# A fused attention, MLP and soft-MoE kernel: the MLP rows of five batches turned by VectorE and DMA for the routing logits

## The chip, the cores and the metric

The kernel runs on one core of a Trainium2 chip. A core has engines that each run their own instruction stream in order and wait for one another by semaphores: TensorE (PE, matmuls and transposes), VectorE (DVE), ScalarE (ACT), GpSimd (POOL) and SyncE (SP, which here issues the DMAs). The metric is the device time of one execution in microseconds (us), the median of the runs.

## The reference

Inputs are f32. Three parts follow one another.

```python
# attention with a small state: x [8,8,512,64], state [8,8,32,64]  (batch, head, token/slot, 64)
a     = softmax(x @ state^T / 8);  xread = a  @ state     # per token, over 32 slots
a2    = softmax(state @ x^T / 8);  sread = a2 @ x         # per slot, over 512 tokens
x     = concat([xread, sread], tokens)                    # -> 8*(512+32) = 4352+256 = 4608 rows of 512

# gated MLP, 512 -> 1536 -> 512
xn    = x / sqrt(mean(x*x) + 1e-6) * rms_g
h     = silu(xn @ w_gate) * (xn @ w_val)                  # [4608,1536]
x     = h @ w_out

# soft MoE: 8 experts with 4 slots each, 32 slots in all
logits = x @ phi                                          # [4608,32]
d      = softmax(logits, over all tokens);  slot_in = d^T @ x
out_e  = relu(slot_in_e @ w1_e) @ w2_e
c      = softmax(logits, over the 32 slots);  result = c @ slot_out
```

## The kernel before

The MLP's output x = h @ w_out is never formed. The kernel folds w_out into phi (`wphi` = w_out @ phi, 1536 x 32), so that logits = h @ wphi, and it sums d^T @ h for the slots, with w_out applied once at the end. The sum over tokens goes batch by batch with a running maximum (`mrun`, `al`, `acc`).

The work is staged by batches of 512 tokens. Stages 0 and 1 work on batches 0 and 1, with the preparation of weights. Then each stage from 2 to 7 is one batch, with 12 units: three chunks c of 512 MLP columns by four tiles t of 128 tokens. A unit is a gate group of six 128x512 matmuls (`main_mm(.., 0)`), silu by ScalarE into `sg` (L496), a value group of six matmuls, and `h` = value x scale x sg by VectorE (L504). Groups write PSUM buffers of the pool `mm` (four); all other products and transposes go through `misc` (three), the logits through `lg` (one). Beside the units, the same engines carry for the next batch its attention: `sT` (token scores), softmaxes (`a`, asum, `e2T`), state reads; the conversion of w_out from its input words (`raw` to `wo` by ScalarE, VectorE and GpSimd, written to DRAM as `w_out`); and the weights of the next chunk times the state (`sw`: `misc<-w,stTg` on TensorE, `wp` by ScalarE L467 and VectorE L468).

The logits need h with its 512 columns on the partitions, since TensorE contracts over the partitions. `h` has tokens there. So `h_T` (L509 to 517) makes four 128x128 transposes on TensorE for a tile (L109), into one misc buffer, which ScalarE copies to `hT` (in units 1 and 2 of a stage VectorE does, L515). Once the four tiles of a chunk are there, `lg_mm` (L519 to 534) multiplies four 128x32 pieces of wphi with the four pieces of hT, each into its own 32 partitions of `lg`, summed over the three chunks. After the last chunk of a batch `post1` copies lg to `lgs`, `post2` sums the four pieces by a matmul and updates the running maximum (`L`, `cmx`), `post_exp` takes the exponential (`E`, `al`), `post3` turns E and L (`ET`, `c_all`), and `slot_h` adds d^T @ h (`misc<-h,ET`).

The order: each unit asks `next_turned` for up to two tiles that are ready (`pend`), turns them and multiplies; `at(u, slot, f)` writes a function into a plan at a unit and one of two slots, and `run(slot)` plays it. The framework's scheduler then orders each engine's stream from that program, so that what is written later may stand earlier. SyncE's DMAs are issued in order from one queue. Big tiles (`h`, `hT`, `raw`, `xT`, ...) come from one pool `k8` of 19 buffers of 128x2048 f32; a tile that takes a buffer waits until the last user of it is done.

## Time and profile before

| | |
|---|---|
| runs, median (lowest to highest) | 671.63 us (671.53 to 674.0) |
| the profiled execution | 673.21 us, its span 671.4 us, clock 0.968 |
| TensorE busy | 622.3 us, 93% of the span, 4448 instructions |
| VectorE busy | 402.4 us, 60% |
| ScalarE busy | 354.8 us, 53% |
| GpSimd busy | 161.2 us, 24% |
| DMA | 92.54 MB, mean 138 GB/s |
| transposes of h on TensorE (L109, with others) | 61.1 us listed, 408 of them |
| gate and value groups (L85, mm) | 307.3 us listed, 1152 matmuls |
| hT copies by ScalarE (L515) | 49.5 us, 86 of them |

Busy is the sum of an engine's instruction times. Matmuls overlap in the pipeline, so what one costs is read from the distance between starts rather than from its own time. The span is the profiled part of one execution; the execution's own time has 1.8 us more. [...] The chain that ended last goes 68% over TensorE, 17% over VectorE, 6% over ScalarE and 3% over DMA.

### The profile page before, as it was taken

What the parts mean: (1) busy time and instruction counts of PE and PEld (TensorE: products, weight loads), DVE (VectorE), ACT (ScalarE), POOL (GpSimd) and SP (SyncE); (2) the same over time, 40 slices, a digit from 0 to 9 for tenths busy, and PEclk for the clock granted to TensorE, in tenths of its full rate; (3) what the DMA queues carried; (4) which work ended last, traced back from release to release, by engine and by line L of the source; (5) the groups of instructions that cost most, each with busy time, mean ns of one, the idle gap of its engine ahead of it and who ended that gap; (6) DMA issues with size and microseconds to landing.
All of it is one profiled execution on the core that took longest, in us unless ns stands there. A gap on an engine that the chain in (4) does not pass through costs nothing.

```text
span 671.4 us, 11241 instructions
## 1 busy us (share of the span) xinstructions
PE 622.3 (93%) x4448; PEld 393.5 (59%) x4448; DVE 402.4 (60%) x831; ACT 354.8 (53%) x599; POOL 161.2 (24%) x172
## 2 busy tenths in 40 slices
PE   6786989999999999999999999999999999999880
PEld 4344556546656766576676657666666777643350
DVE  6969898675398366646835673584554266242170
ACT  5466784566466547445744645485445576211170
POOL 2635364542044003302310340221000000014320
PEclk9698998999999999999999999999899999999995
DMA  9950065132013203202110320300363037999767
GB/s 348 405 221 1 1 250 189 63 130 67 1 49 145 68 0 130 101 1 91 70 68 3 125 95 1 126 6 28 125 252 126 0 120 256 312 355 386 265 228 304
DMA packets 33580, 92.54 MB, mean 138 GB/s; under 512 B 1912, under 2 KB 4088, under 8 KB 30712
## 3 DMA queue, kind: packets, MB, share of 16 engines
q1 hardware_dynamic: 33240, 91.76, 37.3%
q8 instruction: 35, 0.57, 0.4%
q14 instruction: 17, 0.14, 0.1%
q10 hardware_dynamic: 288, 0.07, 0.0%
HBM read 79.76 MB, written 12.06 MB: 137 GB/s over the span
## 4 chain that ended last, share of the span: by engine, by line
PE 68%; DVE 17%; ACT 6%; DMA 3%; issue 2%; POOL 1%; DVEq 0%; POOLq 0%; ACTq 0%
PE mm L85 38%; PE misc L85 18%; PE misc L109 7%; PE lg L85 3%; DMA ew<-in_w_dram 2%; DVE w L208 2%; DVE h L504 2%; DVE asum L322 1%; DVE w L204 1%; DVE wp L468 1%; DVE w L200 1%; ACT sT L298 1%; DVE wo L208 1%; ACT wp L467 1%; ACT a L311 1%
## 5 line engine op out<-in xcount | busy, mean ns | idle before, releaser
L85 PE MATMUL mm<-wp,A 128*128 128x512 f32 x1152 | 307.3, 407 | 2.2 <-ACT sg L496 1.2
L85 PEld LDWEIGHTS mm<-wp,A 128*128 128x128 f32 x1152 | 206.9, 190 | 91.9 <-issue 49.3
L504 DVE SCALAR_TENSOR_TENSOR h<-mm,rinv,sg 128x512 f32<-128x512 f32 x102 | 75.5, 743 | 85.9 <-PE mm L85 78.8
L496 ACT ACTIVATE sg<-mm,rinv 128x512 f32<-128x512 f32 x102 | 70.6, 692 | 81.0 <-PE mm L85 67.3
L467 ACT CAST wp<-misc 128x512 fp32r<-128x512 f32 x96 | 51.8, 590 | 77.2 <-PE misc L85 77.2
L468 DVE TENSOR_TENSOR wp<-misc,wp 128x512 fp32r<-128x512 f32 x96 | 62.0, 684 | 50.5 <-ACT wp L467 50.4
L85 PE MATMUL misc<-w,stTg 64*32 64x512 f32 x768 | 67.5, 627 | 11.2 <-POOL w L212 6.8
L515 ACT COPY hT<-misc 128x512 f32<-128x512 f32 x86 | 49.5, 584 | 39.2 <-PE misc L109 33.1
L109 PE MATMUL misc<-ident,h 128*128 128x128 f32 x408 | 61.1, 275 | 3.7 <-DVE h L504 2.2
L109 PEld LDWEIGHTS misc<-ident,h 128*128 128x128 f32 x408 | 48.0, 140 | 23.3 <-issue 4.1
L85 PE MATMUL misc<-bd,A 128*128 128x256 f32 x192 | 32.1, 306 | 4.4 <-DVE wp L468 2.2
L85 PEld LDWEIGHTS misc<-w,stTg 64*32 64x32 f32 x768 | 11.0, 106 | 42.7 <-POOL w L212 16.7
L212 POOL TENSOR_TENSOR w<-w,raw 128x512 int32<-128x512 int32 x20 | 28.2, 1422 | 30.1 <-issue 9.0
L85 PEld LDWEIGHTS misc<-bd,A 128*128 128x128 f32 x192 | 27.3, 203 | 9.9 <-DVE wp L468 2.6
L441 POOL TENSOR_TENSOR rinv<-ri,rs_magic 128x4 int32<-128x4 int32 (+1 forms) x9 | 1.8, 198 | 130.2 <-DVE ri L437 130.2
L422 ACT ACTIVATE misc<-misc 128x512 f32<-128x512 f32 x32 | 18.7, 584 | 25.7 <-PE misc L85 24.2
L85 PE MATMUL mm<-wh,xsg 128*128 128x512 f32 x96 | 31.7, 399 | 0.0
L212 POOL TENSOR_TENSOR wo<-wo,raw 128x512 int32<-128x512 int32 x18 | 24.3, 1364 | 26.3 <-DVE wo L208 22.1
L269 POOL TENSOR_TENSOR a<-a,rm 128x1024 f32<-128x1024 f32 x7 | 13.4, 1916 | 62.6 <-issue 58.1
L1089 POOL MEMSET sinE<- 128x512 f32 x2 | 1.0, 524 | 111.4 <-PE mm L85 101.2
L325 POOL TENSOR_TENSOR a<-a,asum 128x1024 f32<-128x1024 f32 x7 | 13.4, 1917 | 59.4 <-DVE cs L640 50.1
L85 PE MATMUL lg<-hT,wphi 128*32 128x512 f32 (+1 forms) x216 | 27.5, 578 | 0.0
(203 smaller groups left out, 844.7 us busy)
## 6 DMA issues: line engine op xcount, KB each, us to landing
ew<-in_w_dram SPq DMA_DIRECT2D x27, 1024.0 KB, 7.9
xT<-in_x_t_dram SPq DMA_DIRECT2D x8, 1024.0 KB, 5.1
xn<-in_x_n_dram SPq DMA_DIRECT2D x8, 1024.0 KB, 6.8
raw<-in_w_val_dram SPq DMA_DIRECT2D x6, 1024.0 KB, 16.6
raw<-in_w_out_dram SPq DMA_DIRECT2D x6, 1024.0 KB, 4.9
out_dram<-ob SPq DMA_DIRECT2D x6, 1024.0 KB, 12.9
ew_w<-in_w_dram SPq DMA_DIRECT2D x5, 1024.0 KB, 12.0
raw<-in_w_gate_dram SPq DMA_DIRECT2D x4, 1024.0 KB, 14.3
```

Of the source, the lines that this page charges most:

```text
L85: nc.tensor.matmul(out=o, lhsT=lhsT, rhs=rhs, start=start, stop=stop)
L109: nc.tensor.transpose(o, i, ident)
L208: nc.vector.scalar_tensor_tensor(out=a[:, h], in0=hi[:, h], scalar=-0x40000000, in1=a[:, h], op0=ALU.bitwise_and, op1=ALU.bitwise_or,)
L212: nc.gpsimd.tensor_tensor(out=a[:, h], in0=a[:, h], in1=rnd[:, h], op=ALU.add)
L269: nc.gpsimd.tensor_tensor(out=a3, in0=a3, in1=rm.unsqueeze(2).to_broadcast([P, 32, 32]), op=ALU.subtract)
L325: (eng or nc.gpsimd).tensor_tensor(out=a3, in0=a3, in1=asum.unsqueeze(2).to_broadcast([P, 32, 32]), op=ALU.mult)
L422: nc.scalar.activation(out=ps, in_=ps, func=AF.Square, accum_out=T[b, "ss"][:, t : t + 1])
L467: nc.scalar.copy(t[:, r, 0, :], ps)
L468: nc.vector.tensor_tensor(out=t[:, r, 1, :], in0=ps, in1=t[:, r, 0, :].bitcast(F32), op=ALU.subtract)
L496: nc.scalar.activation(out=sg, in_=ps, func=AF.Silu, scale=RINV[g][:, t : t + 1])
L504: nc.vector.scalar_tensor_tensor(out=HH[g, c][:, t, :], in0=ps, scalar=RINV[g][:, t : t + 1], in1=sg, op0=ALU.mult, op1=ALU.mult,)
L515: (nc.vector.tensor_copy if on_dve else nc.scalar.copy)(HT[g, c][:, :, t * P : (t + 1) * P], ps.rearrange("p (q n) -> p q n", q=4))
```

## The change

For batches 2 to 6 the rows of h are turned without TensorE. `next_turned` hands out two tiles of one chunk at a time. `h_blocks` has VectorE transpose 32x32 blocks of the two tiles (128x1024) into a tile `hB`, with the blocks regrouped so that partition p holds 32-column pieces by block row. When both halves of a chunk are there, `h_move` writes hB by one DMA to a DRAM tile `hD` (1 MB, three buffers) and reads it back by four DMAs of 256 KB, each into 32 partitions of `hT`, which puts the blocks on the partitions where a whole transpose has them. `lg_end` multiplies as before, planned three units later, and reads hT in runs of 32 elements; for the last chunk of a batch it plans `post1` to `slot_h` behind itself. Batches 0, 1 and 7 and the state rows stay with TensorE's transposes.

```diff
--- before.py
+++ after.py
@@ -133,6 +133,7 @@
 
     dram = ctx.enter_context(tc.tile_pool(name="dram", bufs=1, space=bass.MemoryType.DRAM))
     w_out32 = dram.tile([DFF, DM], F32, name="w_out32")
+    hdram = ctx.enter_context(tc.tile_pool(name="hdram", bufs=1, space=bass.MemoryType.DRAM))
     bits = {
         0: w_gate.bitcast(I32), 1: w_val.bitcast(I32), 2: w_out_t.bitcast(I32),
         3: w_out.bitcast(I32),
@@ -516,22 +517,54 @@
             HT[g, c][:, :, t * P : (t + 1) * P], ps.rearrange("p (q n) -> p q n", q=4)
         )
 
+    def by_dma(g):
+        return 2 <= g < B - 1
+
+    HB = {}
+
+    def h_blocks(g, c, t):
+        if t == 0:
+            HB[g, c] = k8("hB")
+        nc.vector.transpose(
+            HB[g, c].rearrange("p g (x i) -> p x g i", i=32)[:, 4 * t : 4 * t + 8],
+            HH[g, c][:, t : t + 2, :].rearrange("p t (q g i) -> p (t q) g i", q=4, g=4),
+        )
+
+    def h_move(g, c):
+        hB = HB.pop((g, c))
+        hT = k8("hT")
+        D = hdram.tile([P, 4, 512], F32, tag="hD", bufs=3, name=f"hD_{g}_{c}")
+        nc.sync.dma_start(out=D, in_=hB)
+        for g_ in range(4):
+            nc.sync.dma_start(
+                out=hT[32 * g_ : 32 * g_ + 32],
+                in_=D[:, g_, :].rearrange("(b i) r -> i b r", b=4),
+            )
+        HT[g, c] = hT.rearrange("p b (t q i) -> p t q b i", q=4, i=32)
+
+    def lg_part(g, c, hT, n):
+        if c == 0:
+            LGP[(g,)] = psp.tile([P, 512], F32, tag="lg", bufs=1, name="lg")
+        lg = LGP[(g,)]
+        for q in range(4):
+            mm(
+                lg[32 * q : 32 * q + 32, : n * P],
+                wphi[:, 4 * c + q, :],
+                hT(q),
+                start=(c == 0),
+                stop=(c == NC - 1),
+            )
+
+    def lg_moved(g, c):
+        hT = HT.pop((g, c))
+        lg_part(g, c, lambda q: hT[:, :, q], NT)
+
     def lg_mm(g, c, t):
         n = gsize(g)
         if t < n - 1:
             return
-        if c == 0:
-            LGP[(g,)] = psp.tile([P, 512], F32, tag="lg", bufs=1, name="lg")
-        lg = LGP[(g,)]
         hT = HT.pop((g, c))
-        for q in range(4):
-            mm(
-                lg[32 * q : 32 * q + 32, : n * P],
-                wphi[:, 4 * c + q, :],
-                hT[:, q, : n * P],
-                start=(c == 0),
-                stop=(c == NC - 1),
-            )
+        lg_part(g, c, lambda q: hT[:, q, : n * P], n)
 
 
     sacc = small("sacc", [P, 1])
@@ -813,6 +846,8 @@
     def next_turned():
         pend.sort()
         now = [it for it in pend[:2] if it[1] in wphi_done and it[0] == pend[0][0]]
+        if now and by_dma(now[0][0]):
+            return now if len(now) == 2 and now[0][1] == now[1][1] else []
         return [] if now and now[0][1:] == (0, 0) and now[0][0] > 0 and now[0][0] - 1 not in ended else now
 
     ended = set()
@@ -823,6 +858,19 @@
             ended.add(now[-1][0])
         return end
 
+    def after_lg(pg, v):
+        ended.add(pg)
+        for u, slot, f in ((0, 2, post1), (1, 1, post2), (1, 1, post_exp), (2, 2, post3)):
+            plan.setdefault((v + u, slot), []).append((f, (pg,)))
+        for i in range(NC):
+            plan.setdefault((v + 4, 1), []).append((slot_h, (pg, i)))
+
+    def lg_end(g, c):
+        lg_moved(g, c)
+        if c == NC - 1:
+            after_lg(g, unit[0])
+
+    unit = [0]
     for s, units in enumerate(stages):
         def at(u, slot, f, *a):
             plan.setdefault((base + u, slot), []).append((f, a))
@@ -948,27 +996,31 @@
 
         for u, (g, c, t) in enumerate(units):
             def run(slot):
-                for f, a in plan.pop((base + u, slot), []):
-                    f(*a)
-
+                while fs := plan.pop((base + u, slot), []):
+                    for f, a in fs:
+                        f(*a)
+
+            unit[0] = base + u
             now = next_turned()
             ps = main_mm(g, c, t, 0)
             sg = main_silu(g, c, t, ps)
+            moved = now and by_dma(now[0][0])
             for it in now:
-                h_T(*it, on_dve=(s > 0 and u in (1, 2)))
+                if not moved:
+                    h_T(*it, on_dve=(s > 0 and u in (1, 2)))
             run(1)
             psv = main_mm(g, c, t, 1)
             main_h(g, c, t, psv, sg)
-            for it in now:
-                lg_mm(*it)
-            if ends(now):
-                pg = now[-1][0]
-                at(u, 2, post1, pg)
-                at(u + 1, 1, post2, pg)
-                at(u + 1, 1, post_exp, pg)
-                at(u + 2, 2, post3, pg)
-                for i in range(NC):
-                    at(u + 4, 1, slot_h, pg, i)
+            if moved:
+                h_blocks(*now[0])
+                if now[1][2] == NT - 1:
+                    h_move(*now[1][:2])
+                    at(u + 3, 2, lg_end, *now[1][:2])
+            else:
+                for it in now:
+                    lg_mm(*it)
+                if ends(now):
+                    after_lg(now[-1][0], base + u)
             run(2)
             pend = pend[len(now) :] + [(g, c, t)]
             if g == B - 2 and u == len(units) - 1:
```

Three places in the order show what moves. On TensorE, at the start of batch 4's stage around the attention transposes (`sT`); before, with A the batch's rows, wp its weights and `misc<-ident,h` the transposes of h:

```order
L85 MATMUL mm<-wp_2894,A_2595 128x512 x6
L85 MATMUL misc<-w_557,stTg 32x512 x8
L85 MATMUL mm<-wp_2839,A_2595 128x512 x6
L109 MATMUL misc<-ident,h_3005 128x128 x4
L85 MATMUL mm<-wp_2894,A_2595 128x512 x6
L109 MATMUL misc<-ident,sT 128x128 x8
L599 MATMUL misc<-ident,E 128x128
L600 MATMUL misc<-ident,L 128x128
L85 MATMUL mm<-wp_2839,A_2595 128x512 x6
L85 MATMUL mm<-wp_2894,A_2595 128x512 x6
L85 MATMUL mm<-wp_3011,A_2595 128x512 x5
```

Here a transpose block of h stands between two groups, and the eight matmuls of w_557 stand together. After the change, the same place of the program (`lg<-hT` of the batch before stands just ahead of it):

```order
L109 MATMUL misc<-ident,sT 128x128 x4
L85 MATMUL mm<-wp_2919,A_2500 128x512
L109 MATMUL misc<-ident,sT 128x128 x4
L85 MATMUL misc<-lgs,r_75 32x128 x4
L85 MATMUL mm<-wp_2919,A_2500 128x512 x3
L85 MATMUL mm<-wp_2955,A_2500 128x512 x6
L85 MATMUL misc<-w_677,stTg 32x512 x4
L85 MATMUL mm<-wp_2919,A_2500 128x512
L85 MATMUL misc<-w_677,stTg 32x512 x4
L85 MATMUL mm<-wp_2919,A_2500 128x512 x5
L85 MATMUL mm<-wp_2955,A_2500 128x512
L85 MATMUL misc<-xn_2945,e2T 32x64 x32
```

The transposes of h are gone, those of E and L no longer stand here, the state-write group of w_677 is in two halves around one gate matmul, and the matmuls on `e2T` come ahead of the value group's rest.

On VectorE, at the same place; before, from the row maximum `cmax` of post3 to the next stage of h:

```order
L606 TENSOR_REDUCE cmax<-misc 128x4
L643 RECIPROCAL cs<-cs 128x4
L504 SCALAR_TENSOR_TENSOR h_3005<-mm,rinv,sg 128x512
L644 TENSOR_TENSOR c_all<-c_all,cs 128x128
L200 TENSOR_SCALAR wo_3133<-wo_3133 128x512 x2
L204 TENSOR_SCALAR wo_3133<-wo_3133 128x512 x2
L208 SCALAR_TENSOR_TENSOR wo_3133<-raw_3044,wo_3133 128x512 x2
L335 COPY e2T<-misc 128x512
L607 TENSOR_TENSOR c_all<-misc,cmax 128x128
L504 SCALAR_TENSOR_TENSOR h_3005<-mm,rinv,sg 128x512
L394 STREAM_TRANSPOSE aT<-a 128x1024
L504 SCALAR_TENSOR_TENSOR h_3235<-mm,rinv,sg 128x512
```

Three h's stand among these rows, and each conversion step (L200, L204, L208) is done for both halves at once. After, from the reciprocal of asum to the second h (`h_3098` is the chunk that starts with unit 4; `h_2909`, of units 0 to 3, stands ahead of this piece, then two `hB` transposes):

```order
L673 TENSOR_SCALAR cs<-cs 128x4
L205 TENSOR_SCALAR wo_3007<-wo_3007 128x512
L676 RECIPROCAL cs<-cs 128x4
L201 TENSOR_SCALAR wo_3007<-wo_3007 128x512
L677 TENSOR_TENSOR c_all<-c_all,cs 128x128
L209 SCALAR_TENSOR_TENSOR wo_3007<-raw_2943,wo_3007 128x512
L205 TENSOR_SCALAR wo_3007<-wo_3007 128x512
L336 COPY e2T<-misc 128x512
L209 SCALAR_TENSOR_TENSOR wo_3007<-raw_2943,wo_3007 128x512
L395 STREAM_TRANSPOSE aT<-a 128x1024
L593 COPY L<-misc 128x128
L594 TENSOR_REDUCE cmx<-misc 128x1
L505 SCALAR_TENSOR_TENSOR h_3098<-mm,rinv,sg 128x512
```

No h stands here any more until L and cmx of the batch before are read, and e2T has come between the two L209.

On SyncE, at the start of a stage; before:

```order
L120 DMA st<-in_st_n_dram 128x128
L162 DMA raw_3044<-in_w_out_dram 128x2x1024
L126 DMA xn_3046<-in_x_n_dram 128x2048
L219 DMA w_out_89<-wo_3133 128x2x512
L119 DMA stT<-in_st_t_dram 128x128
L118 DMA xT_3431<-in_x_t_dram 128x2048
```

Nothing but a small state load stands ahead of `raw`. After, at the same place:

```order
L537 DMA hD_2_2913<-hB_2860 128x2048
L120 DMA st<-in_st_n_dram 128x128
L539 DMA hT_2912<-hD_2_2913 32x4x512 x4
L163 DMA raw_2943<-in_w_out_dram 128x2x1024
L126 DMA xn_2945<-in_x_n_dram 128x2048
L537 DMA hD_0_3102<-hB_3005 128x2048
L220 DMA w_out_89<-wo_3007 128x2x512
L539 DMA hT_3101<-hD_0_3102 32x4x512 x4
L118 DMA xT_3305<-in_x_t_dram 128x2048
```

The loads of `raw` and `xn` now come behind the write of hD and the four reads of hT of the chunk that ended the batch before.

## Rows read from the trace of the kernel before

**Rows 1.** Busy time by window, batch 5; columns: busy, clock, DMA share, GB/s

```profile
373.00:432.40 59.40, 58.90 (x463) 38.80 (x463) 35.77 (x75) 32.62 (x59) 12.44 (x11) 1.00 0.18 63
```

**Rows 2.** TensorE's timeline, start of batch 5; start, length, idle before

```profile
372.95 1.06 PE L85 MATMUL lg<-hT,wphi 128*32 128x512 f32 x8
373.95 1.09 PE L85 MATMUL misc<-w,stTg 64*32 64x512 f32 x16
...
376.46 0.60 PE L109 MATMUL misc<-ident,h 128*128 128x128 f32 x4
376.99 0.43 PE L85 MATMUL misc<-lgs,r 128*32 128x128 f32 x8
...
381.45 0.60 PE L109 MATMUL misc<-ident,h 128*128 128x128 f32 x4
381.81 1.63 PE L85 MATMUL mm<-wp,A 128*128 128x512 f32 x6
383.27 1.04 PE L109 MATMUL misc<-ident,sT 128*128 128x128 f32 x8
...
391.85 0.63 PE L109 MATMUL misc<-ident,h 128*128 128x128 f32 x4 [0.38 <-DVE h L504]
```

**Rows 3.** VectorE's timeline, the same stretch

```profile
375.70 1.29 DVE L468 TENSOR_TENSOR wp<-misc,wp 128x512 fp32r<-128x512 f32 x2 [0.92 <-ACT wp L467]
377.10 0.69 DVE L515 COPY hT<-misc 128x512 f32<-128x512 f32 x1
...
382.70 0.16 DVE L315 TENSOR_SCALAR rs<-s 128x2 f32<-128x2 f32 x1
...
383.53 1.22 DVE L322 TENSOR_REDUCE asum<-a 128x32 f32<-128x1024 f32 x1 [0.48 <-ACT a L311]
...
388.96 1.28 DVE L208 SCALAR_TENSOR_TENSOR wo<-raw,wo 128x512 int32<-128x512 int32 x2
390.17 0.68 DVE L335 COPY e2T<-misc 128x512 f32<-128x512 f32 x1
390.77 0.28 DVE L607 TENSOR_TENSOR c_all<-misc,cmax 128x128 f32<-128x128 f32 x1
390.96 0.74 DVE L504 SCALAR_TENSOR_TENSOR h<-mm,rinv,sg 128x512 f32<-128x512 f32 x1
391.62 1.23 DVE L394 STREAM_TRANSPOSE aT<-a 128x1024 f32<-128x1024 f32 x1
```

**Rows 4.** ScalarE's timeline, the same stretch

```profile
377.37 1.28 ACT L585 ACT_TABLE_LOAD   x1
...
380.07 1.08 ACT L467 CAST wp<-misc 128x512 fp32r<-128x512 f32 x2 [0.82 <-PE misc L85]
...
385.01 0.69 ACT L496 ACTIVATE sg<-mm,rinv 128x512 f32<-128x512 f32 x1
385.60 1.13 ACT L184 ACTIVATE wo<-raw 128x1024 f32<-128x1024 f32 x1
...
388.11 0.70 ACT L496 ACTIVATE sg<-mm,rinv 128x512 f32<-128x512 f32 x1
```

**Rows 5.** DMA issues; columns: count, KB each, median us from issue to landing

```profile
raw<-in_w_out_dram SPq DMA_DIRECT2D x6, 1024.0 KB, 4.9
out_dram<-ob SPq DMA_DIRECT2D x6, 1024.0 KB, 12.9
...
w_out<-wo SPq DMA_DIRECT2D x6, 512.0 KB, 2.8
...
out_dram<-ob SPq DMA_DIRECT2D x6, 256.0 KB, 2.1
```

**Rows 6.** TensorE's timeline in the start-up

```profile
62.57 4.21 PE L85 MATMUL misc<-bd,A 128*128 128x256 f32 x18 [2.16 <-DVE wp L468]
66.71 1.60 PE L85 MATMUL misc<-xn,e2T 128*32 128x64 f32 x50
```

**Rows 7.** Busy time by window, the same place

```profile
60.00:80.00 20.00, 17.26 (x141) 12.72 (x139) 16.50 (x37) 10.64 (x19) 8.48 (x7) 0.83 0.00 1
```

## The prediction

> **What bounds the kernel now.** [...] VectorE and ScalarE each have a dense patch in units 3 to 6, the two softmax parts of the next batch's attention (rs to e2T) with the conversion of w_out [rows 3, 4]; VectorE's average of 60% hides that it is full there. Last I read the DMA issues, for what a megabyte takes [rows 5], and a place where the granted clock is low past the first microseconds [rows 7].
>
> **What TensorE saves.** Batches 2 to 6 have 60 blocks of four transposes, 12 in a stage. What one costs is not its listed 0.60 but the distance to the next start, since the instructions are pipelined: 0.36 us before a gate or value group (381.45 to 381.81) and 0.53 before another small group (376.46 to 376.99) [rows 2]. Eight of 12 in a stage are of the first kind, four of the second: 8 x 0.36 + 4 x 0.53 = 5.0 us, times 5 stages = 25.0. Against it stand about two more changes between kinds of work in a stage (a state-write group cut in halves, the logits cut into a gate group), 0.17 each by the difference of the two spacings: 0.34 x 5 = 1.7. The gap of 0.38 on h goes in about two stages. I take 24 us. The ends are 60 x 0.36 = 21.6 and 60 x 0.60 = 36.
>
> The logits' matmuls stay as many, 1.06 us a chunk [rows 2], but read hT in runs of 32 elements. No row has such a read. If it costs nothing the sum stands; as the other end I take short matmuls, 50 of 64 columns in 1.60 us [rows 6], 0.032 each: eight of these for 512 columns are 0.26 against 1.06/8 = 0.13, so 8 x 0.13 = 1.0 a chunk, 15 us for 15 chunks. I take nothing, since the width of the work is the same, and keep the other end in the range. A gain is excluded: the same columns go through.
>
> **What the other engines get.** VectorE loses two hT copies of 0.69 in a stage and gets six block transposes. The same operation on the same 128x1024 took 1.23 us where it makes aT [rows 3]; here it writes runs of 32. A strided write has a row, the hT copy at 0.69 for half as many elements, so 1.38 at the most; I take 1.23 (the same operation). 6 x 1.23 - 2 x 0.69 = +6.0, or 41.8 of 59.4 us. ScalarE loses ten hT copies in a stage, and pays two more table loads of 1.28 [rows 4], as the exponentials of the token softmax and those of the attention now stand apart. GpSimd's order is unchanged. The new DRAM pool and the loop that empties a slot of the plan issue nothing of their own, and the logits of batch 7 keep their transposes, two a unit from unit 4 on, as many as before. All this costs nothing where TensorE doesn't wait for it. Where it does is the next part.
>
> **The wait that comes in.** In the order of the changed kernel VectorE has no h between h(u3) and h(u4) in batches 3 to 6: two block transposes, the softmax sums, the w_out conversion, e2T, aT and the token maximum all stand ahead of h(u4), where before three h's were let in between. Call T3 the end of value group u3.
> - VectorE: h(u3) is done at T3+0.86 (0.75 and a start); two transposes 2.4, two wp 1.3, lgs 0.65 (a copy like the one at 377.10) make T3+5.2. From rs to the end of e2T (the next start) it took 382.70 to 390.77, 8.07 us before; take away the idle 0.48, one h 0.75, two 128x128 operations of 0.28 that move later, and half of the L208 pair (0.64), since one of the two now stands behind e2T [rows 3]: 5.65. So e2T is done at T3+10.85, and with 0.64, aT 1.16 and the token maximum 0.5 that is T3+13.15.
> - ScalarE: from sg(u3) at T3-0.6 the weight casts to the end of the table load are 380.07 to 385.01, 4.94; another table load 1.28; the w_out work and e2T 385.60 to 388.11, 2.51; sg 0.69 [rows 4]: sg(u4) is done at T3+8.8.
> - TensorE: gate u4 1.5, lg 1.06, value u4 and gate u5 3.0, transposes and lgs 1.3, value u5 1.5, half a state-write group 0.5 [rows 2]: at gate u6 at T3+8.8. It needs sg(u4) there and is just in time; the second half of the state-write group needs a small PSUM buffer that e2T gives back, at T3+10.85, 1.8 us after TensorE is there. The 32 matmuls on e2T wait for the token maximum's buffer, 0.3 more.
> That is 2.15 us in a stage. It happens in batches 3 to 6, which have both softmaxes, so 4 x 2.15 = 8.6. Bounds: nothing if VectorE's spacings close up, and 4.7 a stage if all its instructions take their listed durations end to end, as they don't in [rows 3].
>
> **The DMA chain.** SyncE issues in order. The chunk that ends a batch is written and read back at the start of the next stage, and the loads of w_out (raw) and xn, which had nothing ahead of them, now stand behind that. With T0 the end of the last value group: h and the second block transpose are done at T0+2.1 [rows 3]; the 1 MB write has the 512 KB write to DRAM as nearest row, 2.8 us, twice that 5.6; ends 2.8 (size is free) and 12.9 (the 1 MB write of the output, which stands in a row of its like) [rows 5]. The four reads of 256 KB: 2.1 each, 2.1 together to 8.4 one after another [rows 5], I take 5. So hT lands at T0+12.7. TensorE wants it after nine groups at 1.46, two state-write groups at 1.09 and an lg at 1.06 [rows 2], T0+16.5: 3.8 in hand. raw, 4.9 by itself [rows 5], lands at T0+17.6; ScalarE wants it behind c_all at T3+4.3, and T3 is T0+14.9 (eight groups, two state-write groups, one lg): T0+19.2, 1.6 in hand. I cost the chain at nothing; TensorE's first five units are its cover. Chunks 0 and 1 have three units and more.
> [...] No read into 32 partitions is in this trace.
>
> **Sum.** 673.21 (the profiled execution, 671.4 of it span) - 24 + 8.6 = 657.8. The median of the runs lies 1.6 below the profiled execution, so 656.2; I predict 656.
>
> **Rivals**, each against the median of 671.6.
> 1. *No stall.* VectorE catches up, only the removal counts: 671.6 - 24 = 647.6. For it: 17 us of idle VectorE in a stage [rows 1]; against it, it is not idle in that patch [rows 3].
> 2. *A larger stall.* 4.7 in a stage in place of 2.15: 656.2 + 4 x 2.55 = 666.4. For it: ScalarE's two table loads come just in time only, and sg frees the gate's PSUM.
> 3. *The clock falls at the new stall.* After an idle 2.16 us on VectorE at 62.57 the 18 matmuls that follow took 4.21 us, and the 20 us around it have a clock of 0.83, 0.17 x 20 = 3.4 us lost [rows 6, 7]. If each of four stalls of 2 us costs that, 656.2 + 13.6 = 669.8. Against it: that is one place, in the start-up, and the stage of batch 5 keeps 1.00 through its short gap [rows 1, 2]. [...]
> 4. *The chain is late: slower.* Place: raw behind the four reads at the start of batches 3 to 6. Price: the write takes 12.9 and not 5.6, so raw lands 7.3 later, 5.7 past its need; ScalarE stands before sg(u4), and TensorE at gate u6. 4 x 5.7 = 23: 679. It decides from 1.6 us of lateness on, and is slower than before from about 6 us. For it: SyncE is one queue in order, and two transfers of 1 MB in [rows 5] differ by 8 us. Against it: the DMA engines are idle 82% of the stage [rows 1].
>
> That the change doesn't do what it says is no rival: the order has the transposes gone.
>
> **Chances.** Forecast 0.42, no stall 0.15, larger stall 0.12, clock 0.13, late chain 0.18. What a measurement can tell from no change is 0.5%, 3.4 us here, so 668.3 to 675.0 counts as the same. Forecast, no stall and larger stall are faster (0.69), and of the clock case 0.04, where fewer stages lose it: 0.73. The rest of the clock case (0.09) and a chain late by a little (0.05) are the same: 0.14. The late chain in full is slower: 0.13. The range: 646 at the low end (no stall, with a little more of the removal's upper bound) and 676 at the high end, past the clock case and the strided read at its dearest (656 + 15 = 671); it leaves 0.06 below and 0.12 above. The forecast's own range is 650 to 664.
>
> **What would show it.** In the profile after: stages of batches 3 to 6 near 56.7 us, batch 2 near 54.6 (no stall), TensorE with an idle near 1.8 us before a state-write group in unit 6 that ends on VectorE's e2T, and one of 0.3 before the matmuls on e2T. Block transposes near 1.23 us, lg 1.06 a chunk. Writes to hD near 5.6 us, and no idle before lg and none of ScalarE on raw. The forecast is wrong if the idle time is on a DMA (case 4), if the clock of those stages is under 1.00 (case 3), or if lg takes 2 us.

## The result, and the profile after

| | before | after |
|---|---|---|
| runs, median (lowest to highest) | 671.71 us (671.53 to 674.0) | 681.34 us (680.12 to 684.2) |
| the profiled execution, its span | 673.21, 671.4 | 680.12, 678.3 |
| clock granted to TensorE, mean, as a share of full speed | 0.968 | 0.957 |
| TensorE busy, instructions | 622.3 us, 4448 | 623.0 us, 4208 |
| VectorE, ScalarE busy | 402.4, 354.8 | 437.2, 340.0 |
| DMA | 92.54 MB | 123.98 MB |

The changed kernel is slower: 1.0143 times the time, interval 1.0119 to 1.0166. The forecast was 656, faster. 240 transposes are gone, and yet TensorE is busy as long as before. That is the first thing to explain, and the table of stretches says where. In one kernel below, m2, three of the five executions were over 1.5% longer than the fastest, at a lower clock; its ratio is of the other two, and it has no row in the account. These are three stages of the kernel after, each from one `sT` transpose to the next, with the columns of [rows 1]:

```profile
268.90:328.97 60.07, 57.98 (x412) 34.08 (x411) 42.72 (x80) 29.48 (x52) 12.34 (x10) 1.00 0.58 174
328.97:390.01 61.04, 59.25 (x412) 34.69 (x411) 43.52 (x80) 30.07 (x53) 12.36 (x10) 0.97 0.55 165
390.01:451.02 61.01, 59.22 (x412) 34.80 (x411) 43.51 (x80) 30.08 (x53) 12.35 (x10) 0.97 0.56 164
```

A stage takes 60.1 to 61.0 us in place of 59.4 [rows 1], VectorE has the load that was forecast (43.5; 41.8 was), the DMA share is three times as high, and in two of the three the clock is 0.97. TensorE's own timeline of batch 4's stage shows the rest:

```profile
316.79 1.06 PE L85 MATMUL misc<-w,stTg 64*32 64x512 f32 x8
317.78 0.96 PE L85 MATMUL mm<-wp,A 128*128 128x512 f32 x3
318.67 1.06 PE L85 MATMUL misc<-w,stTg 64*32 64x512 f32 x8
319.67 6.41 PE L85 MATMUL mm<-wp,A 128*128 128x512 f32 x27
...
332.80 1.06 PE L85 MATMUL misc<-w,stTg 64*32 64x512 f32 x8
333.79 0.50 PE L85 MATMUL mm<-wp,A 128*128 128x512 f32 x1
336.08 1.57 PE L85 MATMUL misc<-w,stTg 64*32 64x512 f32 x8 [1.79 <-DVE e2T L336]
337.57 2.72 PE L85 MATMUL mm<-wp,A 128*128 128x512 f32 x6
340.23 1.10 PE L85 MATMUL misc<-xn,e2T 128*32 128x64 f32 x64
...
354.72 1.06 PE L85 MATMUL lg<-hT,wphi 128*32 128x512 f32 x8
...
356.84 1.09 PE L85 MATMUL misc<-w,stTg 64*32 64x512 f32 x16
357.86 3.04 PE L85 MATMUL mm<-wp,A 128*128 128x512 f32 x12
```

Compare the state-write groups (`w,stTg`). Whole, with 16 instructions, one takes 1.02 us to the next start (356.84 to 357.86), as in [rows 2]. Cut in two, each half of eight takes 0.99 (316.79 to 317.78, 318.67 to 319.67). A half costs what the whole costs. In `sw` the first half multiplies partitions 0 to 63 and the second 64 to 127 (the tile of the rows is 64*32), and issued together they run side by side: 16 take 1.02 against 8 in 0.99, and by the trace eight of the 16 are under way in the first 0.26 us of the whole group (from 356.84), four of the eight in the first 0.25 us of a half (from 316.79). The logits' matmuls cost the same 1.0 us a chunk as before, although they read runs of 32.

At 336.08 stands the wait that was forecast, 1.79 us on e2T, and behind it six matmuls take 2.66 us in place of 1.5. The clock of the ten microseconds around the wait, batches 3 to 6, with the columns of [rows 1]:

```profile
272.00:282.00 10.00, 8.69 (x102) 4.83 (x100) 10.00 (x17) 5.85 (x11) 6.65 (x5) 1.00 0.32 87
333.00:343.00 10.00, 8.21 (x95) 4.54 (x88) 10.00 (x17) 5.10 (x7) 6.39 (x5) 0.83 0.35 97
394.00:404.00 10.00, 8.21 (x95) 4.67 (x88) 10.00 (x17) 5.47 (x8) 6.42 (x5) 0.83 0.35 78
455.00:465.00 10.00, 8.21 (x95) 4.78 (x89) 10.00 (x17) 5.76 (x10) 6.43 (x5) 0.83 0.34 91
```

After the wait of batch 3, which is 1.14 us, the clock stays at 1.00; in the other three it is 0.83, so 0.17 x 10 = 1.7 us each, 5.1 together. (A wait of about that size in e1, below, 1.92 us, leaves the clock at 1.00.) VectorE is busy 10.00 of 10.00 there, as forecast. Its timeline and GpSimd's at that place:

```profile
324.83 0.75 DVE L505 SCALAR_TENSOR_TENSOR h<-mm,rinv,sg 128x512 f32<-128x512 f32 x1 [1.97 <-PE mm L85]
...
331.21 0.42 DVE L201 TENSOR_SCALAR wo<-wo 128x512 f32<-128x512 f32 x1
...
332.24 2.05 DVE L201 TENSOR_SCALAR wo<-wo 128x512 f32<-128x512 f32 x1
334.21 0.28 DVE L677 TENSOR_TENSOR c_all<-c_all,cs 128x128 f32<-128x128 f32 x1
...
335.35 0.68 DVE L336 COPY e2T<-misc 128x512 f32<-128x512 f32 x1
335.95 1.16 DVE L209 SCALAR_TENSOR_TENSOR wo<-raw,wo 128x512 int32<-128x512 int32 x1
```

```profile
332.03 1.97 POOL L326 TENSOR_TENSOR a<-a,asum 128x1024 f32<-128x1024 f32 x1 [17.41 <-DVE cs L673]
```

The same instruction took 0.42 and then 2.05 us, the second while GpSimd's 1.97 us multiplication ran: 1.6 us of the patch in which e2T is late. Not all of that is new. In the kernel before, GpSimd's multiplication ran beside `c_all`, which took 1.29 us there and 0.28 after:

```profile
386.40 1.29 DVE L644 TENSOR_TENSOR c_all<-c_all,cs 128x128 f32<-128x128 f32 x1
```

```profile
385.63 1.92 POOL L325 TENSOR_TENSOR a<-a,asum 128x1024 f32<-128x1024 f32 x1 [10.86 <-DVE cs L640]
```

The DMA chain (DMA issues, and the one wait on it in TensorE's list of waits):

```profile
hD<-hB SPq DMA_DIRECT2D x15, 1024.0 KB, 4.3
hT<-hD SPq DMA_DIRECT2D x60, 256.0 KB, 5.7
...
raw<-in_w_out_dram SPq DMA_DIRECT2D x6, 1024.0 KB, 8.3
```

```profile
PE lg L85 <- DMA hT<-hD: 0.9, 1, 0.9
```

The write is faster than was taken (4.3, not 5.6), raw takes 8.3 in place of 4.9 behind the reads, and in the whole run TensorE waits 0.9 us on the chain.

**An account of TensorE.** Taking the distance from each row of TensorE's timeline to the next start, less the idle time shown in brackets, and summing by kind of work from 150 us to the end, gives this against the kernel before. "Pieces" counts, over the 48 state-write groups of the order, the pieces beyond one a group. "Rest" is what remains to the difference of the spans. A wait between the two halves of a whole group has no bracket and stays in the group's cost. The edge at 150 us falls at another place of each order, which can move a cell by up to about 2 us. The later rows are the experiments.

| kernel | pieces | transposes of h | state-write groups | gate and value groups | waits | rest | span | median, ratio |
|---|---|---|---|---|---|---|---|---|
| before | 4 | 39.2 | 40.1 | 232.1 | 6.1 | | 671.4 | |
| after | 20 | -25.4 | +14.9 | +7.5 | +7.9 | +2.0 | +6.9 | 681.3, 1.014 |
| e1_joined | 5 | -24.1 | +6.4 | +5.8 | +16.7 | +5.5 | +10.3 | 681.1, 1.014 |
| e5_raw_early | 20 | -25.3 | +17.2 | +7.2 | +9.2 | +8.5 | +16.8 | 689.5, 1.026 |
| n1_no_dma | 5 | -25.3 | +3.2 | +1.7 | -0.5 | +1.4 | -19.5 | 654.7, 0.976 |
| s1_before_cut | 35 | +0.6 | +29.1 | +0.9 | -2.5 | +1.4 | +29.5 | 706.6, 1.052 |
| m1_misc4 | 9 | -26.1 | +4.3 | +0.2 | +11.0 | +3.3 | -7.3 | 667.7, 0.994 |
| m0_before_misc4 | 4 | -0.8 | -1.5 | -0.9 | -1.1 | -1.4 | -5.7 | 667.4, 0.993 |
| d1_before_traffic | 7 | -0.1 | +0.9 | +5.7 | +19.3 | +2.8 | +28.6 | 703.0, 1.046 |
| e2_late_conv | 11 | -24.1 | +14.4 | +6.0 | +13.5 | +3.2 | +13.0 | 679.7, 1.013 |
| v1_late_logits_conv | 9 | -25.0 | +8.1 | +0.9 | +9.4 | +5.8 | -0.8 | 673.6, 1.002 |
| v2_late_misc4 | 6 | -25.9 | 0.0 | -1.9 | +12.8 | +2.2 | -12.8 | 660.2, 0.981 |
| v0_before_late_conv4 | 4 | -0.9 | -2.4 | -1.2 | -0.7 | -0.4 | -5.6 | 668.7, 0.996 |

For the changed kernel the profiled executions differ by 6.9 us and the medians by 9.6; the account explains the 6.9. Each span is of one execution, in after, s1, n1 and d1 the shortest of its kernel, in e1, e2 and e5 the longest. Of the +7.5 of the gate and value groups in the changed kernel 4.3 came while the clock was under 1.00; the rest lies in groups cut into small pieces, 12 rows of a single matmul in place of 1, 0.38 us each against 0.25 in a row of six.

### The profile page after: what moved, and what is told of

It is laid out like the page before. It is cut to its first block, busy times and chain, and to the rows that moved or that the text cites. A ratio compares the mean times of both kernels' runs of the same rounds, so it can differ in the third digit from the quotient of the medians.

```text
span 678.3 us, 10896 instructions
## 1 busy us (share of the span) xinstructions
PE 623.0 (92%) x4208; PEld 373.0 (55%) x4208; DVE 437.2 (64%) x849; ACT 340.0 (50%) x559; POOL 160.8 (24%) x172
## 2 busy tenths in 40 slices
DMA packets 44380, 123.98 MB, mean 183 GB/s; under 512 B 3113, under 2 KB 5289, under 8 KB 39593
## 4 chain that ended last, share of the span: by engine, by line
PE 66%; DVE 13%; ACT 4%; DMA 2%; issue 2%; POOL 1%; SPq 0%; DVEq 0%; ACTq 0%; POOLq 0%
PE mm L85 39%; PE misc L85 18%; PE misc L109 4%; PE lg L85 3%; PE so L85 2%; DVE wo L201 2%; DVE wp L469 1%; DVE hB L528 1%; DMA raw<-in_w_out_dram 1%; DVE wo L209 1%; DVE asum L323 1%; DMA hT<-hD 1%; DVE h L505 1%; ACT wp L468 1%; DVE wo L205 1%
## 5 line engine op out<-in xcount | busy, mean ns | idle before, releaser
L85 PE MATMUL mm<-wp,A 128*128 128x512 f32 x1152 | 312.7, 414 | 2.3 <-ACT sg L497 1.2
L85 PEld LDWEIGHTS mm<-wp,A 128*128 128x128 f32 x1152 | 212.2, 193 | 116.4 <-issue 62.1
L85 PE MATMUL misc<-w,stTg 64*32 64x512 f32 x768 | 83.7, 621 | 17.3 <-DVE e2T L336 9.0
L85 PEld LDWEIGHTS misc<-w,stTg 64*32 64x32 f32 x768 | 12.9, 105 | 46.5 <-issue 18.5
L528 DVE STREAM_TRANSPOSE hB<-h 128x1024 f32<-128x1024 f32 x30 | 37.1, 1237 | 0.3
L516 ACT COPY hT<-misc 128x512 f32<-128x512 f32 x38 | 21.4, 588 | 24.2 <-PE misc L109 18.2
L85 PE MATMUL misc<-h,ET 128*32 128x512 f32 x204 | 26.6, 596 | 0.6 <-DVE e2T L336 0.4
## 6 DMA issues: line engine op xcount, KB each, us to landing
xn<-in_x_n_dram SPq DMA_DIRECT2D x8, 1024.0 KB, 10.3
```

Of the source, the lines that this page charges most:

```text
L85: nc.tensor.matmul(out=o, lhsT=lhsT, rhs=rhs, start=start, stop=stop)
L516: (nc.vector.tensor_copy if on_dve else nc.scalar.copy)(HT[g, c][:, :, t * P : (t + 1) * P], ps.rearrange("p (q n) -> p q n", q=4))
L528: nc.vector.transpose(HB[g, c].rearrange("p g (x i) -> p x g i", i=32)[:, 4 * t : 4 * t + 8], HH[g, c][:, t : t + 2, :].rearrange("p t (q ...
```

## The experiments

The theory: the removal gives its 25 us, and is more than paid for by 16 more cut state-write groups at about 0.95 each, by the wait for e2T, and by the clock behind it. Rivals: the DMA traffic slows the work, the DMA chain is late, or the transposes' removal is hidden. In the expectations theory A, or the halves theory, is that half a group takes as long as the whole; B, that a cut costs 0.17 and the loss is traffic; C, that what joining saves comes back as a longer wait for e2T.

**A cut by itself: s1_before_cut.** The kernel before, nothing of the change in it; `half(r)` is one half of a group, and the second is pinned behind the next gate or value group:

```diff
-        for r in range(2):
-            ps = misc()
...
+        half(0)
+        if b > 1:
+            halves_due.append(half)
...
             ps = main_mm(g, c, t, 0)
+            while halves_due:
+                halves_due.pop(0)(1, True)
```

> The kernel before, with the second half of each state-write group from batch 2 on (and of some before) put behind the next gate or value group: 35 pieces beyond one a group in place of 4. No DMA is added and the transposes of h stay. Theory A: 31 x 0.99 = 30.7 us more, near 702. Theory B (0.17 a cut): 5 more, near 677. If the halves cost only where DMAs move data into the array's inputs: no change, 672.

Measured: 706.6 us, ratio 1.0517 (1.0483 to 1.055). TensorE's timeline of it, a half, a value group, the other half:

```profile
333.37 1.06 PE L463 MATMUL misc<-w,stTg 64*32 64x512 f32 x8
334.36 1.65 PE L85 MATMUL mm<-wp,A 128*128 128x512 f32 x6
335.94 1.06 PE L463 MATMUL misc<-w,stTg 64*32 64x512 f32 x8
336.94 0.66 PE L109 MATMUL misc<-ident,h 128*128 128x128 f32 x4
```

Each half takes 0.99 or 1.00, and the account says +29.1 us for 31 cuts, 0.94 each, with no DMA added. The price of a cut is shown; 0.17 is off by more than five times. The median rose by 35, more than the 29.5 of the profiled execution; the runs of this kernel lie between 702.7 and 707.8.

**No round trip: n1_no_dma.** In `h_move` the tile, its write and its four reads are left out:

```diff
-        hT = k8("hT")
-        D = hdram.tile([P, 4, 512], F32, tag="hD", bufs=3, name=f"hD_{g}_{c}")
-        nc.sync.dma_start(out=D, in_=hB)
-        for g_ in range(4):
-            nc.sync.dma_start(...)
+        hT = hB
```

> The changed kernel without the DRAM round trip: the logits' matmuls read hB where it lies (so the logits are not the reference's), no hD writes and no hT reads, and raw has nothing ahead of it. The order has the state-write groups whole (5 pieces beyond one a group) and e2T ahead of the conversion. Theory A with the wait as the rest: 671.7 - 25.4 (transposes) + 1 to 3 of small gaps = 647 to 650. If VectorE's block transposes by themselves hold TensorE up: 655 or more. If the transposes' removal was hidden behind something else all along: 668 to 672.

Measured: 654.7, ratio 0.9756 (0.9737 to 0.9774). A stretch of it, with the columns of [rows 1]:

```profile
310.00:370.00 60.00, 59.50 (x440) 36.23 (x424) 44.27 (x83) 33.54 (x57) 12.54 (x10) 1.00 0.24 86
```

VectorE carries all its transposes (44.27 of 60) and TensorE is busy 59.50 at a clock of 1.00. The time is some 5 us above what was expected, at the edge of the second answer. Much of the difference is in four groups that are whole in the order and yet take twice their time:

```profile
273.21 2.05 PE L85 MATMUL misc<-w,stTg 64*32 64x512 f32 x16 [0.16 <-DVE wp L469]
```

Its second half starts 0.98 us after the first, released by VectorE's `srd`. The group takes 1.98 to the next start in place of 1.02, in four stages, 3.8 us together. So the removal is worth its 25.3, VectorE holds TensorE up by little more than these 3.8 (whether by the block transposes is not shown), and what the change loses comes with the round trip, its DMAs and its tile hT, which this kernel leaves out together.

**The halves kept together: e1_joined.** In `sw` both buffers are taken first, and a one-column matmul claims the second:

```diff
+        pss = [misc(), misc()]
+        for r, hp, n in [(1, 0, 1)] + [(r, hp, 512) for r in range(2) for hp in range(4)]:
+            ins = nc.tensor.matmul(out=pss[r][32 * hp : 32 * hp + 32, :n], ...)
+            if n > 1 and b > 1:
+                tc.keep_in_program_order(ins)
```

> The changed kernel, with the two halves of each state-write group (the weights times the state; r=0 on partitions 0 to 63, r=1 on 64 to 127) kept together in TensorE's order from batch 2 on: a one-column matmul claims the second PSUM buffer first, then the eight follow one another. The DMAs and VectorE's order stay, with the wait for e2T. Pieces beyond one a group over the run: 20 in the changed kernel, 5 here, 4 in the kernel before. Theory A (the two halves run side by side on the two halves of the array's rows, so that half alone takes as long as the whole, 0.99 us): 15 x 0.99 = 14.9 us less, near 666. Theory B (what was predicted: a cut costs a change of 0.17, and the loss is matmuls slowed by the DMA traffic): 15 x 0.17 = 2.6 less, near 679. Theory C (what is saved here is lost in a longer wait for e2T, as TensorE comes there earlier): about 4 x 1 us less than A gives, near 670.

Measured: 681.1, ratio 1.0135 (1.0097 to 1.0173), no gain. The state-write groups cost 8.5 less than in the changed kernel (+6.4 against +14.9; the claims themselves take 2.8), and the waits 8.8 more. TensorE's timeline:

```profile
337.87 0.22 PE L461 MATMUL misc<-w,stTg 64*32 64x1 f32 x2
...
341.16 1.09 PE L461 MATMUL misc<-w,stTg 64*32 64x512 f32 x16 [1.92 <-DVE e2T L336]
```

The group is whole (16 at 341.16), and waits for the same e2T as before, since VectorE's order is the same; the claim holds a buffer while it waits. Theory C, with more waits than it gave. Behind this wait of 1.92 us, one of three, the clock does not fall:

```profile
338.00:348.00 10.00, 5.99 (x96) 3.46 (x95) 10.00 (x17) 5.59 (x10) 6.48 (x5) 1.00 0.32 87
```

The kernel tells of the halves only that joining them shortens them; it doesn't make the run shorter.

**The load of raw a stage earlier: e5_raw_early.**

```diff
-                at(4 if g == 1 else 1, 1, wload, 1)
+                if g == 1:
+                    at(4, 1, wload, 1)
+                if g < 6:
+                    at(9 - o, 1, wload, 1)
```

> The changed kernel, with the load of raw (for the w_out conversion) issued in unit 9 of the stage before, so that it stands ahead of the last hD write and hT reads. e2T now comes ahead of the conversion steps on VectorE; the state-write groups are still cut (20 pieces beyond one a group, as many as in the changed kernel). If the wait for e2T cost its 6.9 us and brought the granted clock down behind it (0.83 over 10 us in three stages, 1.7 us each, 5.1 in all), and nothing takes its place: 681.3 - 6.9 - 5.1 = 669. If the wait is only moved on to the next buffer on VectorE or ScalarE: 677 to 681. If the conversion's lateness was on the path by its DMA and not by the order: also 669, but with the idle time on raw in the changed kernel, which its trace doesn't show.

Measured: 689.5, ratio 1.0261 (1.0233 to 1.0289), slower than any of the three answers. TensorE's list of waits (total us, times, longest):

```profile
PE misc L632 <- ACT E L613: 7.1, 4, 2.0
...
PE misc L85 <- DVE e2T L336: 4.4, 3, 3.2
```

Past the start-up the wait for e2T is down from 6.9 to 0.4 us, and ScalarE's E takes its place, four times up to 2.0 us: 7.1. More groups were cut too: the account's rest has +4.6 for the logits and +3.8 for the token scores (`misc<-xT,stT`), which the order cuts now. The lateness of raw was not what cut the groups, since 20 pieces stay with raw early.

**A fourth small PSUM buffer: m1_misc4, and its control m0_before_misc4.** One line, in the changed kernel and in the kernel before:

```diff
-        return psp.tile([P, 512], F32, tag="mm", bufs=4, name="mm")
+        return psp.tile([P, 512], F32, tag="mm", bufs=3, name="mm")
...
-        return psp.tile([P, 512], F32, tag="misc", bufs=3, name="misc")
+        return psp.tile([P, 512], F32, tag="misc", bufs=4, name="misc")
```

> The changed kernel with one buffer of PSUM moved: the small pool has four in place of three, the pool of the gate and value groups three in place of four. The state-write groups come out whole but for one a stage: 9 pieces beyond one a group in place of 20 (4 in the kernel before). VectorE's order around e2T stays, so the wait for it should stay. Halves theory: 11 x 0.99 = 10.9 us less than the changed kernel, 670. Rival (the time went to the DMA traffic, or to the wait and the clock alone): 679 to 682. If three buffers are too few for the gate and value groups, more than 682, with idle time on silu or h.

> The kernel before with the same move of a PSUM buffer (four small, three for the gate and value groups), as a control: its state-write groups are whole already (4 pieces beyond one a group, as without). Halves theory: no change, 670 to 673. If the extra small buffer is worth something by itself, by more than the 3.4 us that can be told: under 668.

Measured: m1 667.7, ratio 0.9938 (0.9917 to 0.9959); m0 667.4, ratio 0.993 (0.9909 to 0.995). The changed kernel gains 13.6, the kernel before 4.9, so about 9 of it are what the buffer does for the change, with 11 cuts fewer; its state-write groups cost 10.6 less. The control was expected to stand still and didn't: the buffer is worth something by itself. The change with it is worth nothing: 667.7 against 667.4. What is left in m1 (list of waits):

```profile
PE misc L85 <- DVE e2T L336: 4.3, 4, 2.5
PE mm L85 <- DVE h L505: 4.1, 5, 2.1
PE misc L632 <- ACT E L613: 4.0, 4, 1.1
PE lg L85 <- DMA hT<-hD: 2.3, 1, 2.3
```

Past the start-up the wait for e2T is down to 1.9 us, and waits for E (4.0), for one read of hT (2.3) and for h (1.8) have come in its place. The gate and value groups cost what they cost before (+0.2), so the waits are what is left: +11.0.

**The conversion late: e2_late_conv, and with four small buffers m2_misc4_late_conv.**

```diff
-                at(6 if g == 1 else 2, 2, wconv, 1)
+                at(6 if g == 1 else 7, 2, wconv, 1)
```

> The changed kernel with one number changed: the w_out conversion in unit 7 of a stage in place of 2. e2T stands ahead of it on VectorE. 11 pieces beyond one a group in place of 20. Halves theory, wait and clock: 681.3 - 9 x 0.99 - 6.9 - 5.1 = 660. If the wait moves to the next small buffer: 667 to 672. If raw's late landing was what held the kernel up: 681 or more, since raw comes as late as before.

> As the kernel with four small buffers, and the w_out conversion moved from unit 2 of a stage to unit 7, so that e2T stands ahead of it on VectorE. 8 pieces beyond one a group. Halves theory and the wait as second part: 670 of the kernel with four small buffers, less 7 us of wait and 5 of low clock behind it: 658. If the wait only moves to another small buffer, as it did with the early load of raw: 665 to 670. Either is below the kernel before, if the halves theory holds.

Measured: e2 679.7, ratio 1.0132 (1.0081 to 1.0184), close to its third answer, but past the start-up no wait is on raw. m2 took 665.7 and 668.9, ratio 0.993 (0.9899 to 0.9961), no better than its control, the kernel before with the same buffer (m0). TensorE's waits in e2:

```profile
PE misc L632 <- DVE srd L357: 10.5, 4, 2.6
...
PE lg L85 <- DMA hT<-hD: 3.6, 1, 3.6
```

e2T comes in time, and the next small buffer is late instead, that of `srd`, by 2.6 us in each of four stages: the wait moved on and grew. The groups' cost stays at +14.4 with only 11 pieces, because several whole ones wait inside for their second buffer (16 instructions in 1.66 us at 302.23, the second half released by VectorE's `wp`), and four took 1.95 to 2.36 us (the clock of this execution is 0.952). Moving one instruction out of the patch on VectorE doesn't empty the patch.

**The traffic alone: d1_before_traffic.** The kernel before, with this in `lg_mm` for batches 2 to 6:

```diff
+            h2 = k8("hT2")
+            D = hdram.tile([P, 4, 512], F32, tag="hD", bufs=3, name=f"hD_{g}_{c}")
+            nc.sync.dma_start(out=D, in_=HT[g, c])
+            for g_ in range(4):
+                nc.sync.dma_start(out=h2[32 * g_ : 32 * g_ + 32], in_=...)
```

> The kernel before with the DMA traffic of the change alone: for batches 2 to 6 each finished hT is written to DRAM and read back by four transfers into a tile that nobody uses, with raw and xn queued behind the last of them as in the changed kernel. Transposes and copies stay. 7 pieces beyond one a group in place of 4. Halves theory, with the traffic itself free: 671.5 + 3 = 674.5. Rival (matmuls are slowed by the traffic, or raw comes late): 679 or more, with the gate and value groups' own time longer or idle time on raw.

Measured: 703.0, ratio 1.0458 (1.044 to 1.0477). That is in the rival's range, far above 674.5, but without the rival's signs, as the following shows. Its waits:

```profile
PE misc L85 <- DVE wp L469: 8.7, 10, 2.2
PE mm L85 <- ACT wp L468: 7.8, 5, 2.6
```

The transposes (-0.1) and the state-write groups (+0.9 with three more pieces) take what they took, so the traffic does not slow these. The gate and value groups have +5.7, but not by slower matmuls: a row of six takes 1.49 us to the next start, as in the kernel before, and the difference is in cut groups (18 single matmuls in place of 1) and, for 0.9 of it, in the clock. Past the start-up no wait is on raw. The 19.3 us are waits, most of them for the next chunk's weights, which are cast just before they are needed. Three waits of ScalarE and VectorE at those casts (1.9 and 2.1 us in all) end on a read of hT from DRAM, whose buffer the weights take, so the big buffers have become scarce; how much of the 19 is that and how much another order of the casts isn't settled. This kernel doesn't separate the traffic from the buffers, and so refutes only that traffic slows the matmuls.

**The logits and the conversion late: v1_late_logits_conv and v2_late_misc4.** In the changed kernel (v2 with m1's line as well), the four logits' matmuls also pinned behind what was written before them:

```diff
-                    at(u + 3, 2, lg_end, *now[1][:2])
+                    at(u + 5, 2, lg_end, *now[1][:2])
...
-                at(6 if g == 1 else 2, 2, wconv, 1)
+                at(6 if g == 1 else 6, 2, wconv, 1)
```

> The changed kernel with three small PSUM buffers as it had, the logits' matmuls five units behind their chunk in place of three (pinned behind the work written before them), and the w_out conversion in unit 6 of a stage in place of 2. VectorE then has e2T ahead of the token softmax and of the conversion, and two h's before the token maximum. State-write groups: 9 pieces beyond one a group in place of 20. Halves theory with the wait and the clock behind it as the rest: 681.3 - 11 x 0.99 - 6.9 (wait) - 5.1 (clock) = 658. If the wait comes back elsewhere, as it did in two runs: 664 to 670. Rival (the DMA chain itself holds the kernel up): 679 to 682.

> As the kernel with late logits and late conversion, and four small PSUM buffers with three for gate and value groups. 6 pieces beyond one a group. 3 x 0.99 less than that kernel, and the 4.9 us that the fourth small buffer gave the kernel before: 650 to 655. If three buffers for gate and value groups make TensorE wait for h or silu where VectorE is full: as much as that kernel or more, 658 to 664, with idle time on h.

Measured: v1 673.6, ratio 1.0016 (1.0 to 1.0031); v2 660.2, ratio 0.9814 (0.9788 to 0.984). v2 beats both kernels. Both are slower than was expected; v2 lies in its second answer, but without the idle time on h that was its sign. A stretch of it, and TensorE's timeline there:

```profile
310.00:370.00 60.00, 57.06 (x424) 35.62 (x423) 41.07 (x80) 30.51 (x52) 12.56 (x10) 1.00 0.63 187
```

```profile
315.75 1.83 PE L85 MATMUL mm<-wp,A 128*128 128x512 f32 x6 [1.25 <-ACT wp L468]
318.36 1.36 PE L109 MATMUL misc<-ident,sT 128*128 128x128 f32 x8 [0.79 <-ACT sT L299]
...
320.13 1.09 PE L85 MATMUL misc<-w,stTg 64*32 64x512 f32 x16
321.15 2.58 PE L85 MATMUL mm<-wp,A 128*128 128x512 f32 x10
323.66 1.10 PE L85 MATMUL misc<-xn,e2T 128*32 128x64 f32 x64
```

The state-write groups are whole (16 in 1.02), e2T holds nothing up, the waits here are of 1.25 us and less, and the clock is 1.00, with a DMA share of 0.63. It still loses 12.8 us to more waits, half of the removal.

**A control for v2: v0_before_late_conv4.** The kernel before, with four small buffers and the conversion in unit 6.

> Control for the kernel with late logits, late conversion and four small buffers (660.2): the kernel before with the same two settings that don't belong to the change, the w_out conversion in unit 6 and four small PSUM buffers. 4 pieces beyond one a group, transposes of h kept. If turning the rows by VectorE and DMA is worth what is left of its 25 us after waits, this stays at 665 to 670, some 7 us above that kernel. If the gain of that kernel came from the two settings alone: 658 to 662.

Measured: 668.7, ratio 0.9963 (0.9949 to 0.9977), so turning the rows by VectorE and DMA is worth 8.5 us (668.7 - 660.2; about 10 by the ratios to the kernel before) where the order is good. The two settings alone don't give the gain of v2. Its later, pinned logits have no control: the kernel before was not run with them.

## Why the prediction was wrong

- *What TensorE saves* was right: 25.0 forecast, 25.4 measured. Counting these as microseconds of the run rests on TensorE being busy 58.90 us of the stage's 59.40 [rows 1], with one gap of 0.38 [rows 2]; n1, with 25.3 off its transposes, has a span shorter by 19.5. The logits' matmuls cost nothing more in runs of 32 (+0.1), as taken. The dear end of that term, 15 us, was misread: the 50 matmuls in 1.60 us stand in the stretch with a clock of 0.83 [rows 6, 7], and 64 of the same kind take 1.10 at 340.23.
- *The step that failed* is the sentence behind it: "about two more changes between kinds of work in a stage (a state-write group cut in halves, the logits cut into a gate group), 0.17 each", 1.7 us. The term was mis-sized twice. The price: a half costs as much as the whole, 0.94 to 0.99 (s1, and the rows at 316.79), since its other half was free only beside it. The count: the order of the changed kernel has three cut groups in a steady stage, 16 over the run, not one. The whole term of 1.7 was +14.9 in the state-write groups alone. The price stood in the trace of before, in the start-up, where halves stand alone:

```profile
43.36 1.06 PE L85 MATMUL misc<-w,stTg 64*32 64x512 f32 x8
44.35 1.66 PE L85 MATMUL mm<-wp,A 128*128 128x512 f32 x6
```

  Eight in 0.99, against 16 in 1.02 in [rows 2]. The spacing of another instruction (a transpose, 0.17) was taken for a price that a row of the very same one gave.
- *The wait* was right in place and cause. Its size, 1.85 worked out for e2T (2.15 less 0.3) against 1.79 in three stages and 1.14 in batch 3, is partly luck. With h(u3) done at 325.58 for T3+0.86, e2T was done at T3+11.2 and not 10.85, and TensorE was there at T3+9.6 (334.29) and not 8.8, most of it by the half group, priced at 0.5 and taking 0.99. Both came late, and the difference hides it. The text's own times, 10.85 less 8.8, give 2.05 where it says 1.8. 8.6 was forecast for four stages, 6.5 came on e2T. The 0.3 before the matmuls on e2T did not come.
- *The clock*, a rival with 0.13, came with the wait as well, not in its place: three of four stages, 1.7 each and not 3.4. It could have been a term beside the wait, with a chance of its own, but not a sure one: behind the 1.92 of e1 the clock stayed.
- *The DMA chain* was right: no wait on raw, 0.9 us on hT in all. But the chain sets the order: without it (n1) there are 5 pieces and no wait for e2T in the stages of batches 3 to 6. The round trip's price is paid in the order, not in a wait for its data; that too few small buffers make that order is supported by m1 (a fourth takes 11 of 16 cuts away), not shown for every cut.
- The sum: -24 + 8.6 was forecast, -25.4 (transposes) + 14.9 (state-write groups) + 7.9 (all waits) + 7.5 (gate and value groups, 4.3 of it the clock) + 2.0 (rest) = +6.9 came out. The last 3.2 of gate and value groups, cut into small pieces, had no term either.

What stays open: why the scheduler cuts the groups exactly where it does (an earlier raw takes no cut away); how much of d1's waits is the big buffers; and why the clock fell behind 1.79 us in the changed kernel and not behind 1.92 in e1.

## What to carry to other kernels

Where an order is to be compared, price each group whose shape changes by a row of the same shape, and count over the whole run: matmuls on 64 of the 128 partitions were all but free beside those on the other 64 here (16 in 1.02 us) and cost the full time alone (8 in 0.99). Even a group that is whole in the order can lose this, when its second buffer comes late (1.98 in n1). An instruction taken off the bounding engine is worth only what the new order leaves of it, so look at what else the scheduler moved before at the thing that was removed. The clock can be down behind a stall (0.83 over ten microseconds behind three waits of 1.79 us in the changed kernel, 1.00 behind one of 1.92 in e1), so price both, and give the second a chance.

## What the runs showed of the hardware that was not expected

- Behind a wait of 1.79 us in a full stream the granted clock was down three times of three (0.83 over ten microseconds; 0.50 from 337 to 339 us), behind one of 1.14 it stayed at 1.00; six matmuls took 2.66 us behind one in place of 1.5. The length of the wait alone doesn't decide it: one of 1.92 us in e1 left the clock at 1.00, and of four of 1.31 us in d1 it was down behind two (0.97 over those stages, five matmuls in 2.25 and 2.24 us; 1.57 behind another).
- A VectorE instruction of 0.42 us took 2.05 beside a GpSimd multiplication of 1.97. That is 1.6 us lost; what the two engines share is not shown. The kernel before has 1.0 of it, on `c_all` (1.29 in place of 0.28).
- One PSUM buffer moved from the gate and value groups to the small pool gave the kernel before 4.9 us (m0).
